# Attention plus feed-forward on one core: reordered ScalarE and VectorE work in the first tile, and moved steps of k and q

## The chip, the cores and the metric

The kernel runs on one core of a Trainium2 chip. TensorE multiplies, VectorE and ScalarE do the elementwise work, GpSimd takes a few elementwise steps, and SyncE issues the transfers. Each engine works through its own queue in order and waits at its head for what the next instruction needs. The metric is the device time of one execution in microseconds; 921.27 us is the median of three runs before the change (919.81 to 922.92).

## The reference

For each of 8 batches and 8 heads (576 positions, head size 64), `softmax` of q over the head dimension multiplies the matrix `softmax(k over positions)^T v`. The 4608 x 512 result x goes through a feed-forward layer of width 2048:

```
q_s = exp(q - max(q, -1)) / (sum(...) + 1e-9)          # over the 64 of a head
k_s = exp(k - max(k, axis=2)) / (sum(...) + 1e-9)      # over the 576 positions
x   = q_s @ (k_s^T v)                                  # per batch and head
h   = x @ w_in                                         # 4608x512 @ 512x2048
g   = max(h, 0) + log1p(exp(-|h|))                     # softplus
out = g @ w_out                                        # 4608x2048 @ 2048x512
```

All of it is fp32.

## The kernel before

**Tiles and slots.** The 4608 tokens are cut into nine tiles of 512 (`SUBS`), and the 2048 hidden columns into 16 blocks (`NJ`). A slot n is one pair (tile t, block j), n = 16 t + j. In a slot TensorE computes `up(t, j)` (L372 onwards) into a PSUM buffer `ph`, of which there are two, then `down` of the block two slots earlier into four accumulators `po`, then the products that other steps have left in the list `waiting`. Softplus of the slot (L387 to L402) is four ScalarE passes (|h|, exp, 1+u, ln) and three VectorE passes (L399 to L401). L400 reads `ph` and is the last reader of it, so `up` two slots on can overwrite the buffer only behind it.

**First tile.** In tile 0 matrices are multiplied in fp32: each matmul has two instructions in the trace, eight for an `up` and eight for a `down`. The weights come from memory as 64-bit words, and are put together while tile 0 runs, two blocks ahead: `top_w` (L122) and `scale_w` (L117) on ScalarE and `sign_w` (L128) on VectorE make the parts of block j+2 in slot j, `join_w` (L138) on VectorE joins those of block j+1 in slot j. `up` of a block needs its join. From tile 1 on the products are made of two rounded parts each (three matmuls for one); the weights are split for that once by `split_w` (L147 on ScalarE, L148 on VectorE), one block in each slot that `SPLITS` lists. The part of block k overwrites the raw words of block k-1, and block k must be split before slot 16+k. g is split in tile 1 and later by `split_g` (L406 on ScalarE, L407 on VectorE).

**Attention one tile ahead.** While tile t-1 runs, the steps of batch t and tile t are spread over its slots by `attend(t)`; `lazy(make, slots)` puts the i-th step of a unit in the slot that `slots` names. Lists `first`, `steps` and `last` hold what is issued in a slot: `first` and `steps` ahead of the split and of softplus, `last` behind softplus. For batches 1 and 2 (`ON_PE`) a unit of k and v is: `top` (L184, maximum over positions on VectorE, then a transpose on TensorE), `across` (L200, then a second transpose), `shift` (L205 on VectorE), `product` (exponential L211 on ScalarE, then 10 x 2 small matmuls L216 on TensorE), `scale` (L226, L227) and `split` (L240 on ScalarE, L243 on VectorE). There are two buffers `kvt` for k and v; the products of unit h release one, and behind them `kv_next` issues the load of the unit two further on (L169 and L172), whose `top` is the first to read it. The unit of q has twelve steps: two maxima (L280), a join, two shifts (L292), two exponentials (L295), two sums (L298), an inversion (L302, L303) and two divisions (L306). For tile 1 the shifts and divisions run on GpSimd, later on VectorE. The unit of x (L323, L329, L330, products L337 to L339, L349, L350) follows in the last slots of a tile.

**Order.** All of it stands under `tc.manual_schedule()`: each engine gets its instructions in the order in which the loop at the end of the function issues them.

Of the kernel before, what the change touches and what calls it, by code (L numbers as in the profile page):

```python
# [8 lines left out]
F32 = mybir.dt.float32  # L9
# [7 lines left out]
ALU = mybir.AluOpType  # L17
AX = mybir.AxisListType

P = 128  # L20
# [15 lines left out]
ON_PE = 2  # L36
START = [P * sum(SUBS[:t]) for t in range(len(SUBS) + 1)]
NTILE = len(SUBS)

SPLITS = [10, 11, 12, 13, 14, 15, 16, 17, 18, 19, 20, 21, 22, 23, 24, 25]  # L40
TOK = P * max(SUBS)
assert START[-1] == NT

# [13 lines left out]
def tile_attn_ffn(  # L57
# [9 lines left out]
    nc = tc.nc  # L67
# [4 lines left out]
    tp = ctx.enter_context(tc.tile_pool(name="tp", bufs=1))  # L72
# [15 lines left out]
    ln1 = const.tile([P, 1], F32, name="ln1")  # L88
# [7 lines left out]
    def load_w(k):  # L96
        raw[k] = wp.tile([P, 2, DM], I64, name=f"w{k}")
        nc.sync.dma_start(out=raw[k][:, 0], in_=w_in[k])
        nc.sync.dma_start(out=raw[k][:, 1], in_=w_out[k])
# [157 lines left out]
    def q_load(t):  # L257
        qt = qp.tile([P, HP * TOK], F32, name="qt")
        nc.sync.dma_start(out=qt, in_=q[:, HP * START[t]:HP * START[t + 1]])
        qtiles[t] = qt.rearrange("p (h n) -> p h n", h=HP)  # L260
# [126 lines left out]
    def softplus(t, j, ph):  # L387

        if t == 0:

            u, w = (tp.tile([P, TOK], F32, name=("u", "w", "l")[(2 * j + i) % 3]) for i in range(2))
            l = gp.tile([P, TOK], F32, name=("g_hi", "g_lo")[j % 2])
        else:
            u, w, l = (tp.tile([P, TOK], F32, name=name) for name in ("u", "w", "l"))
        nc.scalar.activation(u, ph, AF.Abs)  # L395
        nc.scalar.activation(u, u, AF.Exp, scale=-1.0)  # L396
        nc.scalar.activation(w, u, AF.Copy, bias=1.0)  # L397
        nc.scalar.activation(l, u, AF.Ln, bias=1.0)  # L398
        nc.vector.scalar_tensor_tensor(out=w, in0=w, scalar=1.0, in1=u, op0=ALU.subtract, op1=ALU.subtract)  # L399
        nc.vector.scalar_tensor_tensor(out=w, in0=ph, scalar=0.0, in1=w, op0=ALU.max, op1=ALU.subtract)  # L400
        nc.vector.scalar_tensor_tensor(out=l, in0=l, scalar=ln1, in1=w, op0=ALU.subtract, op1=ALU.add)  # L401
        return l  # L402

    def split_g(l):
        g_hi, g_lo = (gp.tile([P, TOK], F32R, name=name) for name in ("g_hi", "g_lo"))
        nc.scalar.copy(g_hi, l)  # L406
        nc.vector.tensor_tensor(out=g_lo, in0=l, in1=g_hi.bitcast(F32), op=ALU.subtract)  # L407
        return g_hi, g_lo
# [44 lines left out]
    def kv_prefetch(**place):  # L453
        if ahead[0] < len(kv_order):
            bh = kv_order[ahead[0]]
            loaded[bh] = kv_load(*bh, **place)
            ahead[0] += 1

    with tc.manual_schedule():

        make_identity(nc, ident)
        q_load(0)
        for i in range(HP):
            place = dict(pool=xp, tag=f"x{i - 1}", shape=(P, HP * TOK)) if i >= 2 else {}
            kv_prefetch(engine=nc.vector, queue=nc.scalar, **place)
        for k in range(5):
            load_w(k)
        nc.vector.memset(zero, 0.0)

        nc.scalar.activation(ln1, zero, AF.Ln, bias=1.0)  # L470
        whole = wp.tile([P, HP, P], F32, name="spare")
        qT = wp.tile([P, HP, TOK], F32, name=f"w{NJ - 1}")
        x0 = xp.tile([P, HP, TOK], F32, name="x0")
        for z in [whole] + [z.bitcast(F32) for i in range(2) for z in kv_hi[i] + kv_lo[i]]:
            nc.vector.memset(z, 0.0)

        po = [ps_o.tile([P, DM], F32, name=f"po{h}") for h in range(HP)]
        units = [kv_unit(0, h, po[h]) for h in range(HP)]  # L480
        first = [x_first(h, po[h]) for h in range(HP)]
        todo = {f"q{i}": fn for i, fn in enumerate(q_unit(0))}
        for h in range(HP):
            todo.update({f"u{h}{i}": fn for i, fn in enumerate(units[h])})
            todo.update({f"x{h}{i}": fn for i, fn in enumerate(first[h])})
        for k in range(3):
            for name, fn in (("t", top_w), ("m", scale_w), ("s", lambda k: sign_w(k, nc.gpsimd)), ("j", join_w)):
                todo[f"{name}{k}"] = lambda k=k, fn=fn: fn(k)

        warm = ps_h.tile([P, TOK], F32, name="ph")  # L490
        todo["warm"] = lambda: [nc.tensor.matmul(warm[:, 0:P], lhsT=ident, rhs=ident, start=True, stop=True) for _ in range(8)]
        todo["kv"] = kv_prefetch
        todo["w"] = lambda: [load_w(k) for k in range(5, 10)]
        todo["q"] = lambda: q_load(1)
        for name in (
            "q0 q1 u00 q2 q3 q4 q5 u10 u01 u11 u02 u12 q6 u03 u13 u20 u30 u21 u31 u22 u32 t0 m0 s0 u23 u33 warm q7 q8 q9 "
            "kv kv w u04 u14 u05 u15 q10 q11 x00 x10 x01 x11 t1 m1 u24 u34 u25 u35 x20 x30 x21 x31 s1 j0 x02 x12 x22 x32 "
            "t2 m2 s2 j1 q"
        ).split():
            todo[name]()  # L500

        def attend(t):

            steps = [[] for _ in range(NJ + 1)]
            first, last = ([[] for _ in range(NJ)] for _ in range(2))

            def lazy(make, slots):
                unit = []

                def step(i):  # L510
                    def fn():
                        if not i:
                            unit.extend(make())
                        unit[i]()
                    return fn

                for i, s in enumerate(slots):
                    where, s = s if isinstance(s, tuple) else (steps, s)
                    where[s].append(step(i))

            if t < B:
                for h in range(HP):
                    if t <= ON_PE:
                        slots = [2 * h + i for i in (0, 1, 2, 3, 4, 4)]
                    else:

                        g, z = 5 * (h // 2), h % 2
                        slots = [g + i for i in (z, z + 1, z + 1, 3, 4, 4)]
                    lazy(lambda h=h: kv_unit(t, h, banks[h % 2], after=kv_next), slots)
            lazy(lambda: q_unit(t), (3, 4, 5, 5, 6, 7, 8, 7, 8, 9, 9, 10) if t == 1 else (2, 3, 3, 4, 5, 6, 6, 7, 8, 8, 9, 10))  # L530
            for h in range(HP):
                a = h + 11
                lazy(
                    lambda h=h: x_unit(t, h, banks[h % 2]),
                    [a, a, a, a + 1 if h < 2 else NJ] if t == 1 else
                    [a, (last, a), (first, a + 1), (last, a + 1) if h < 2 else NJ],
                )
            if t + 1 < NTILE:
                steps[14].append(lambda: q_load(t + 1))
            return steps, first, last  # L540

        order = [(t, j) for t in range(NTILE) for j in range(NJ)]
        pending, soft, waiting = [], None, []
        for n in range(len(order) + 3):
            slot = order[n] if n < len(order) else None
            if slot:
                t, j = slot
                if j == 0:
                    steps, first, last = attend(t + 1) if t + 1 < NTILE else [[[] for _ in range(NJ + 1)]] * 3
                ph = up(t, j)  # L550
                if t == 0 and 1 < j + 1 < NJ:
                    join_w(j + 1)
                for fn in first[j] + steps[j]:
                    fn()
                if t == 0 and 1 <= j <= HP:
                    split_whole(j - 1)
                if n in SPLITS:
                    split_w(SPLITS.index(n))
                if j == NJ - 1:
                    for fn in steps[NJ]:  # L560
                        fn()
            if soft:
                pending.append((soft[0], split_g(soft[1]) if soft[0][0] else soft[1]))
                soft = None
            if slot:
                soft = slot, softplus(t, j, ph)
                if t == 0 and 2 < j + 2 < NJ:
                    for fn in (top_w, scale_w, sign_w):
                        fn(j + 2)
                for fn in last[j]:  # L570
                    fn()
            while pending and order.index(pending[0][0]) <= n - 2:
                (t, j), g = pending.pop(0)
                down(t, j, g)
            for products in waiting:
                products()
            waiting.clear()
# [37 lines left out]
```

## Time and profile before

| what | value |
|---|---|
| median of three runs | 921.27 us |
| the profiled execution, its own time | 920.85 us |
| its span, first to last instruction | 919.1 us |
| TensorE / VectorE / ScalarE / GpSimd busy | 883.2 / 700.7 / 582.7 / 67.0 us |
| granted TensorE clock, mean | 0.991 |

Times in a timeline are counted from the span's start. A row gives start and duration in us, the engine, the line of the kernel, the operation, what it writes and reads with shapes, the number of instructions merged in the row, and in square brackets how long the engine had been idle and what ended that. A start that comes a little before the end of the row ahead is the engine's pipeline.

### The profile page before, as it was taken

The numbers are of one execution on the slowest core, as the hardware profiler recorded it, in microseconds if no ns is written. First come the engines' busy times: TensorE is split into PE (matmuls) and PEld (weight loads), VectorE is DVE, ScalarE is ACT, GpSimd is POOL, SyncE is SP. The second block draws the span as 40 slices with busy tenths as digits, with TensorE's granted clock in tenths as the row PEclk, the third lists the DMA queues.
The fourth block names the chain that finished last, engine by engine and source line by source line (L and its number), as shares of the span: only waits on it lengthen the run. The fifth ranks groups of instructions, "written<-read, shape, count | busy, mean of one in ns | idle before, by whom it ended". The sixth has DMA issues, their size and how long they took to land.

```text
span 919.1 us, 11673 instructions
## 1 busy us (share of the span) xinstructions
PE 883.2 (96%) x4196; PEld 680.2 (74%) x4196; DVE 700.7 (76%) x1094; ACT 582.7 (63%) x982; POOL 67.0 (7%) x119
## 2 busy tenths in 40 slices
PE   3799989989999999999999999999999999999998
PEld 2343444667788888888888888888888888888886
DVE  8798878788778877887688768976897676765553
ACT  4666566767656665666576657665675566656554
POOL 2302300000000100020002000100110000000000
PEclk9899989999999999999999999999999999999999
DMA  9945101111013101301130113011200110001001
GB/s 313 381 141 195 52 0 47 46 53 32 21 46 98 36 17 47 98 23 30 46 98 9 44 46 98 1 52 46 84 16 1 46 47 1 1 1 47 0 1 46
DMA packets 49034, 55.28 MB, mean 60 GB/s; under 512 B 2256, under 2 KB 39120, under 8 KB 47824
## 3 DMA queue, kind: packets, MB, share of 16 engines
q1 hardware_dynamic: 48400, 54.27, 17.9%
q8 instruction: 33, 0.54, 0.2%
q10 hardware_dynamic: 576, 0.26, 0.1%
q14 instruction: 25, 0.20, 0.1%
HBM read 45.09 MB, written 9.44 MB: 59 GB/s over the span
## 4 chain that ended last, share of the span: by engine, by line
PE 83%; DVE 8%; ACT 5%; issue 2%; DMA 1%; POOL 0%; SPq 0%; DVEq 0%; ACTq 0%; POOLq 0%
PE ph L382 12%; PE po L427 12%; PE po L429 12%; PE po L428 12%; PE ph L383 12%; PE ph L384 12%; PE ph L377 3%; PE po L423 3%; PE att L216 2%; DVE w L138 1%; DVE w L128 1%; PE att L339 1%; PE att L338 1%; PE att L337 1%; DMA kvt<-in_kv_tail 1%
## 5 line engine op out<-in xcount | busy, mean ns | idle before, releaser
L429 PE MATMUL po<-w,g_lo 128*128 128x512 f32 x480 | 187.2, 390 | 1.9 <-DVE g_lo L407 1.9
L382 PE MATMUL ph<-x,w 128*128 128x512 f32 x480 | 188.8, 393 | 0.0
L427 PE MATMUL po<-w,g_hi 128*128 128x512 f32 x480 | 187.6, 391 | 0.0
L383 PE MATMUL ph<-x,w 128*128 128x512 f32 x480 | 186.9, 389 | 0.0
L428 PE MATMUL po<-w,g_hi 128*128 128x512 f32 x480 | 186.9, 389 | 0.0
L384 PE MATMUL ph<-x,w 128*128 128x512 f32 x480 | 186.8, 389 | 0.0
L399 DVE SCALAR_TENSOR_TENSOR w<-w,u 128x512 f32<-128x512 f32 x134 | 92.5, 690 | 117.1 <-ACT w L397 116.9
L406 ACT CAST g_hi<-l 128x512 fp32r<-128x512 f32 x128 | 79.5, 621 | 137.1 <-DVE l L401 134.9
L395 ACT ACTIVATE u<-ph 128x512 f32<-128x512 f32 x134 | 80.2, 598 | 55.6 <-PE ph L384 50.7
L401 DVE SCALAR_TENSOR_TENSOR l<-l,ln,w 128x512 f32<-128x512 f32 x128 | 96.3, 752 | 14.6
L429 PEld LDWEIGHTS po<-w,g_lo 128*128 128x128 f32 x480 | 90.1, 188 | 21.7 <-DVE g_lo L407 2.7
L382 PEld LDWEIGHTS ph<-x,w 128*128 128x128 f32 x480 | 90.4, 188 | 19.7 <-issue 0.6
L384 PEld LDWEIGHTS ph<-x,w 128*128 128x128 f32 x480 | 90.1, 188 | 19.0
L427 PEld LDWEIGHTS po<-w,g_hi 128*128 128x128 f32 x480 | 90.2, 188 | 18.0
L383 PEld LDWEIGHTS ph<-x,w 128*128 128x128 f32 x480 | 90.2, 188 | 17.9
L428 PEld LDWEIGHTS po<-w,g_hi 128*128 128x128 f32 x480 | 90.1, 188 | 17.8
L407 DVE TENSOR_TENSOR g_lo<-l,g_hi 128x512 fp32r<-128x512 f32 x128 | 87.1, 680 | 15.5 <-ACT g_hi L406 14.1
L400 DVE SCALAR_TENSOR_TENSOR w<-ph,w 128x512 f32<-128x512 f32 x134 | 92.6, 691 | 4.6
L397 ACT ACTIVATE w<-u 128x512 f32<-128x512 f32 x134 | 84.8, 633 | 4.2
L396 ACT ACTIVATE u<-u 128x512 f32<-128x512 f32 x134 | 84.7, 632 | 4.3
L398 ACT ACTIVATE l<-u 128x512 f32<-128x512 f32 x128 | 79.2, 619 | 12.5 <-DVE g_lo L407 12.5
L377 PE MATMUL ph<-x,w 128*128 128x512 f32 x128 | 61.6, 627 | 0.0
(136 smaller groups left out, 1020.7 us busy)
## 6 DMA issues: line engine op xcount, KB each, us to landing
kvt<-in_kv SPq DMA_DIRECT2D x30, 512.0 KB, 4.8
qt<-in_q SPq DMA_DIRECT2D x9, 1024.0 KB, 4.8
w<-in_w_in SPq DMA_DIRECT2D x16, 512.0 KB, 8.1
w<-in_w_out SPq DMA_DIRECT2D x16, 512.0 KB, 8.9
out<-w SPq DMA_DIRECT2D x32, 256.0 KB, 2.3
kvt<-in_kv_tail SPq DMA_DIRECT2D x28, 64.0 KB, 4.5
x<-in_kv SPq DMA_DIRECT2D x2, 512.0 KB, 9.4
out<-x SPq DMA_DIRECT2D x4, 256.0 KB, 2.4
```

The source lines that it names most:

```text
L377: nc.tensor.matmul(ph, lhsT=y[:, h * P:(h + 1) * P], rhs=x0[:, h], start=h == 0, stop=h == HP - 1)
L382: nc.tensor.matmul(ph, lhsT=w_hi, rhs=x_hi, start=h == 0, stop=False)
L383: nc.tensor.matmul(ph, lhsT=w_lo, rhs=x_hi, start=False, stop=False)
L384: nc.tensor.matmul(ph, lhsT=w_hi, rhs=x_lo, start=False, stop=h == HP - 1)
L397: nc.scalar.activation(w, u, AF.Copy, bias=1.0)
L399: nc.vector.scalar_tensor_tensor(out=w, in0=w, scalar=1.0, in1=u, op0=ALU.subtract, op1=ALU.subtract)
L400: nc.vector.scalar_tensor_tensor(out=w, in0=ph, scalar=0.0, in1=w, op0=ALU.max, op1=ALU.subtract)
L401: nc.vector.scalar_tensor_tensor(out=l, in0=l, scalar=ln1, in1=w, op0=ALU.subtract, op1=ALU.add)
L407: nc.vector.tensor_tensor(out=g_lo, in0=l, in1=g_hi.bitcast(F32), op=ALU.subtract)
L427: nc.tensor.matmul(po, lhsT=g_hi[:, ms], rhs=w_hi, start=j == 0, stop=False)
L428: nc.tensor.matmul(po, lhsT=g_hi[:, ms], rhs=w_lo, start=False, stop=False)
L429: nc.tensor.matmul(po, lhsT=g_lo[:, ms], rhs=w_hi, start=False, stop=j == NJ - 1)
```

## The change

It has five parts.

1. `SPLITS`: the sixteen weight splits go from slots 10 to 25 to slots 6 to 13, 16 to 19, 21, 23, 25 and 27.
2. In tile 0 softplus issues only L399 in its own slot; L400 and L401 (`rest`) are issued in the next slot, behind that slot's steps and split. The buffers are named accordingly: `u` is always the same one, `w` alternates between two.
3. In tile 0 the three conversions of block j+2 are issued ahead of softplus, and behind `rest` of the slot before.
4. For the k and v units of batches 1 and 2, `top` goes to the list `first` of its slot, and `shift` from slot 2h+2 to slot 2h+3, where the exponential is.
5. For q of tile 2 the steps' slots go from (2, 3, 3, 4, 5, 6, 6, 7, 8, 8, 9, 10) to (1, 2, 3, 4, 5, 5, 6, 6, 7, 8, 9, 10).

```diff
-SPLITS = [10, 11, 12, 13, 14, 15, 16, 17, 18, 19, 20, 21, 22, 23, 24, 25]
+SPLITS = [6, 7, 8, 9, 10, 11, 12, 13, 16, 17, 18, 19, 21, 23, 25, 27]
...
-            u, w = (tp.tile([P, TOK], F32, name=("u", "w", "l")[(2 * j + i) % 3]) for i in range(2))
+            u, w = (tp.tile([P, TOK], F32, name=name) for name in ("u", ("w", "l")[j % 2]))
...
         nc.vector.scalar_tensor_tensor(out=w, in0=w, scalar=1.0, in1=u, op0=ALU.subtract, op1=ALU.subtract)
-        nc.vector.scalar_tensor_tensor(out=w, in0=ph, scalar=0.0, in1=w, op0=ALU.max, op1=ALU.subtract)
-        nc.vector.scalar_tensor_tensor(out=l, in0=l, scalar=ln1, in1=w, op0=ALU.subtract, op1=ALU.add)
-        return l
+
+        def rest():
+            nc.vector.scalar_tensor_tensor(out=w, in0=ph, scalar=0.0, in1=w, op0=ALU.max, op1=ALU.subtract)
+            nc.vector.scalar_tensor_tensor(out=l, in0=l, scalar=ln1, in1=w, op0=ALU.subtract, op1=ALU.add)
+            return l
+
+        return rest
...
-                        slots = [2 * h + i for i in (0, 1, 2, 3, 4, 4)]
+                        slots = [(first, 2 * h)] + [2 * h + i for i in (1, 3, 3, 4, 4)]
...
-            lazy(lambda: q_unit(t), (3, 4, 5, 5, 6, 7, 8, 7, 8, 9, 9, 10) if t == 1 else (2, 3, 3, 4, 5, 6, 6, 7, 8, 8, 9, 10))
+            if t == 1:
+                slots = 3, 4, 5, 5, 6, 7, 8, 7, 8, 9, 9, 10
+            elif t <= ON_PE:
+                slots = 1, 2, 3, 4, 5, 5, 6, 6, 7, 8, 9, 10
+            else:
+                slots = 2, 3, 3, 4, 5, 6, 6, 7, 8, 8, 9, 10
+            lazy(lambda: q_unit(t), slots)
...
-                pending.append((soft[0], split_g(soft[1]) if soft[0][0] else soft[1]))
+                pending.append((soft[0], split_g(soft[1]) if soft[0][0] else soft[1]()))
                 soft = None
             if slot:
-                soft = slot, softplus(t, j, ph)
+
                 if t == 0 and 2 < j + 2 < NJ:
                     for fn in (top_w, scale_w, sign_w):
                         fn(j + 2)
+                l = softplus(t, j, ph)
+                soft = slot, l() if t else l
```

## Rows read from the trace of the kernel before

**Rows 1.** The head of the profile's page: the span, and busy time of each engine with its share and its instructions.

```profile
span 919.1 us, 11673 instructions
PE 883.2 (96%) x4196; PEld 680.2 (74%) x4196; DVE 700.7 (76%) x1094; ACT 582.7 (63%) x982; POOL 67.0 (7%) x119
```

**Rows 2.** The view of stretches, one of them in the third tile: its bounds and length, then busy time and instructions of TensorE, its weight loads, VectorE, ScalarE and GpSimd, granted clock, share of the DMA engines, GB/s.

```profile
300.00:400.00 100.00, 100.00 (x520) 83.04 (x519) 80.34 (x128) 65.47 (x114) 9.50 (x18) 1.00 0.14 45
```

**Rows 3.** The view of waits, TensorE only, whole span: who waited for whom, us in total, times, longest.

```profile
PE att L337 <- DVE q_lo L330: 5.6, 4, 2.6
PE att L186 <- DVE mx L184: 4.6, 3, 2.1
...
PE att L201 <- DVE m L200: 2.1, 1, 2.1
```

**Rows 4.** The timeline of TensorE in the first tile: `up` of slots 7, 8, 9 and 15 (L377), the transpose ahead of the first of them and the first product of x (L337) ahead of the last.

```profile
82.51 0.33 PE L186 MATMUL att<-ident,mx 128*128 128x128 f32 x1 [2.09 <-DVE mx L184]
82.67 5.30 PE L377 MATMUL ph<-x,w 128*128 128x512 f32 x8
...
92.40 3.60 PE L377 MATMUL ph<-x,w 128*128 128x512 f32 x8
...
99.44 3.59 PE L377 MATMUL ph<-x,w 128*128 128x512 f32 x8
...
153.33 0.30 PE L337 MATMUL att<-q_hi,kv_hi 128*128 128x64 f32 x1 [1.11 <-DVE q_lo L330]
...
154.38 3.60 PE L377 MATMUL ph<-x,w 128*128 128x512 f32 x8
```

**Rows 5.** The timeline of VectorE in the first tile: the joins (L138) of slots 1, 4, 5, 10, 11 and 14 (the first and the last of 14, among others), and L401 of slot 9.

```profile
41.20 1.22 DVE L138 SCALAR_TENSOR_TENSOR w<-w 128x1024 uint32<-128x1024 uint32 x1
...
59.70 1.23 DVE L138 SCALAR_TENSOR_TENSOR w<-w 128x1024 uint32<-128x1024 uint32 x1
...
69.39 1.23 DVE L138 SCALAR_TENSOR_TENSOR w<-w 128x1024 uint32<-128x1024 uint32 x1
...
107.43 1.47 DVE L401 SCALAR_TENSOR_TENSOR g_lo<-g_lo,ln,w 128x512 f32<-128x512 f32 x1
...
110.17 2.72 DVE L138 SCALAR_TENSOR_TENSOR w<-w 128x1024 uint32<-128x1024 uint32 x1
...
120.95 1.23 DVE L138 SCALAR_TENSOR_TENSOR w<-w 128x1024 uint32<-128x1024 uint32 x1
...
150.01 1.23 DVE L138 SCALAR_TENSOR_TENSOR w<-w 128x1024 uint32<-128x1024 uint32 x1
```

**Rows 6.** The timeline of GpSimd: the second division of q for tile 1.

```profile
108.88 2.93 POOL L306 TENSOR_TENSOR qt<-qt,s 128x1024 f32<-128x1024 f32 x1
```

**Rows 7.** The groups of VectorE's instructions in the first tile (33 to 160 us), shapes kept apart: count, busy us, mean ns of one, idle time before them.

```profile
L148 DVE TENSOR_TENSOR w<-w,w 128x1024 fp32r<-128x1024 f32 x5 | 6.1, 1223 | 1.3 <-ACT w L147 1.3
L184 DVE TENSOR_REDUCE mx<-kvt 128x128 f32<-128x640 f32 x4 | 5.2, 1302 | 0.0
...
L205 DVE TENSOR_TENSOR kvt<-kvt,att 128x640 f32<-128x640 f32 x4 | 3.3, 821 | 0.1
```

**Rows 8.** The page's list of costly groups: VectorE's three steps of softplus.

```profile
L399 DVE SCALAR_TENSOR_TENSOR w<-w,u 128x512 f32<-128x512 f32 x134 | 92.5, 690 | 117.1 <-ACT w L397 116.9
...
L401 DVE SCALAR_TENSOR_TENSOR l<-l,ln,w 128x512 f32<-128x512 f32 x128 | 96.3, 752 | 14.6
...
L400 DVE SCALAR_TENSOR_TENSOR w<-ph,w 128x512 f32<-128x512 f32 x134 | 92.6, 691 | 4.6
```

**Rows 9.** The timeline of ScalarE in slot 4: L240 of k's unit, the first pass of softplus, the two conversions.

```profile
61.28 0.63 ACT L240 ACTIVATE kv_hi<-att,r 64x64 fp32r<-64x64 f32 x2 [3.11 <-DVE r L227]
...
62.26 0.60 ACT L395 ACTIVATE l<-ph 128x512 f32<-128x512 f32 x1
...
64.61 1.13 ACT L122 ACTIVATE w<-w 128x1024 uint32<-128x1024 uint8 x1
65.64 1.15 ACT L117 ACTIVATE w<-w 128x1024 f32<-128x1024 f32 x1
```

**Rows 10.** The groups of ScalarE's instructions in the first tile, columns as in rows 7.

```profile
L147 ACT CAST w<-w 128x1024 fp32r<-128x1024 f32 x5 | 5.6, 1113 | 0.0
...
L211 ACT ACTIVATE kvt<-kvt 128x640 f32<-128x640 f32 x4 | 2.9, 729 | 0.0
...
L295 ACT ACTIVATE qt<-qt 128x1024 f32<-128x1024 f32 x2 | 2.1, 1049 | 0.0
```

**Rows 11.** The timeline of SyncE's queue: the second transfer of the load that unit 0 of batch 1 releases, and the first one of that which unit 0 of batch 2 releases.

```profile
58.62 0.67 SPq L172 DMA_DIRECT2D kvt<-in_kv_tail  x1
...
186.37 0.55 SPq L169 DMA_DIRECT2D kvt<-in_kv  x1
```

**Rows 12.** The view of transfers between 57.9 and 64 us: count, KB, us from issue to landing.

```profile
kvt<-in_kv_tail SPq DMA_DIRECT2D x1, 64.0 KB, 3.8
```

**Rows 13.** The timeline of VectorE in the second tile: the first instruction of slot 20's steps, k's maximum in that slot, L399 of slot 27, and the step behind that slot's softplus.

```profile
188.41 0.15 DVE L226 TENSOR_SCALAR r<-att 128x1 f32<-128x1 f32 x1
...
191.39 1.32 DVE L184 TENSOR_REDUCE mx<-kvt 128x128 f32<-128x640 f32 x1 [0.43 <-DMA kvt<-in_kv_tail]
...
239.77 0.69 DVE L399 SCALAR_TENSOR_TENSOR w<-w,u 128x512 f32<-128x512 f32 x1 [1.14 <-ACT w L397]
...
241.97 0.68 DVE L330 TENSOR_TENSOR q_lo<-att,q_hi 128x512 fp32r<-128x512 f32 x1
```

## The prediction

> **What bounds the kernel now.** I read the page's head first: TensorE is busy 883.2 of 919.1 us (96%), VectorE 700.7 [rows 1]. Then the stretches: from 300 to 400 us TensorE is busy all 100.00 us at clock 1.00 [rows 2]. Nothing in the diff reaches slots behind the second tile, so what can be won is TensorE's idle time in the first two tiles. The view of waits puts it at 5.6 + 4.6 + 2.1 = 12.3 us for three kinds of wait, every one ended by VectorE [rows 3]. A wait can cost more than itself: behind the wait of 2.09 us the eight passes of an `up` take 5.30 us instead of 3.60, which is half clock for part of them, 1.7 us more [rows 4]. The ceiling of any gain is thus some 14 to 18 us.
>
> So the first two tiles run at the pace of VectorE with ScalarE, and TensorE follows. I measure that pace by VectorE's rounds: from the start of one slot's join to the start of the next one's. From slot 1 to slot 14 the joins start at 41.20 and 150.01 [rows 5], 13 rounds in 108.81 us, in order 5.3, 6.8, 6.4, 9.7, 6.7, 9.9, 8.0, 9.2, 7.0, 10.8, 9.3, 9.9, 9.9. TensorE alone needs 7.04 us for a slot without attention (92.40 to 99.44 [rows 4]). Prices below are start to start, some 0.1 us under the durations of rows 7 to 10.
>
> **First tile, what is won.** In slot 0, L400 and L401 (0.69 + 0.75 [rows 8]) leave the place ahead of slot 1's join, which then starts at 39.7 instead of 41.2: 1.5 won. Slots 1 and 2 are shorter by 0.1 and 0.7 (k's shift goes out of slot 2, 0.82 [rows 7]).
>
> With the conversions first, the chain of a slot through ScalarE changes its end. Before, four passes and two conversions (62.26 to 65.64, and the second conversion's 1.1 [rows 9]) end in `sign_w`, some 1.3, and the join. After, conversions and three passes end in L399, 0.7, and the join. That is 0.5 (ln) + 0.6 = 1.1 less wherever the chain decides: slots 8 and 10 to 13. Slots 11, 12 and 13 become 8.2, 8.85, 8.85. Slot 10 (110.17 to 120.95, 10.78 [rows 5]) also loses the 1.5 by which its join is stretched (2.72 against 1.23): 8.0. Slot 8 takes a split's cast (1.05 [rows 10]) into the chain and stays at 9.1.
>
> **First tile, what it costs.** The maximum of k (L184) goes ahead of all other steps, and VectorE waits at its head for the load. In slot 4 that is the load issued behind the products of slot 3: its second transfer goes out at 58.62 [rows 11] and lands 3.8 later [rows 12], at 62.4. With TensorE 0.85 earlier that is 61.55, and VectorE is there at 59.8. The round of 9.69 loses the shift (0.74) and gains 1.75 of waiting: 10.7. In slots 3, 5, 7 and 9 the shift now stands in the slot of its exponential (0.73 [rows 10]), so ScalarE's queue, with conversions and softplus, waits behind VectorE. Slot 3: 1.14 join + 0.76 shift + 0.66 exponential + 0.3 cast of k^T v + 2.1 conversions + 1.95 three passes + 0.72 L399 = 7.65. Slot 5: GpSimd's shift of q holds L401, 8.2. Slot 6, with a split and without the shift: 9.9. Slot 7, as slot 3 with q's exponential (1.05 [rows 10]) and a cast of 1.05 for the one of 0.3: 9.5.
>
> Slot 9: its 7.0 loses a hold of 0.7 (L401 1.47 instead of 0.75 [rows 5, 8]) and gains a shift (0.74) and a split (1.12 [rows 7]). The split comes while GpSimd divides q. No row shows L148 beside GpSimd; the nearest are L401 and L138, two SBUF inputs each, and L138 ended 1.08 behind GpSimd's end (110.17 + 2.72 against 108.88 + 2.93 [rows 5, 6]). Its price lies between 0 and 2.2 (GpSimd's instruction from start to end); I take 2.1, as of L138. The round becomes 10.3. The Trainium skill ("SBUF — State Buffer", section "SBUF: two separate sides") says that a VectorE operation with two SBUF inputs and a GpSimd operation that reads SBUF exclude each other for a whole instruction. By that rule L148 is held and the sum stands; if only scalar_tensor_tensor were held, the first tile would end 2 us earlier.
>
> The 13 rounds: 5.2 + 6.1 + 7.65 + 10.7 + 8.2 + 9.9 + 9.5 + 9.1 + 10.3 + 8.0 + 8.2 + 8.85 + 8.85 = 110.55, so slot 14's join starts at 150.3, against 150.01.
>
> TensorE loses more, since L400 of a slot now comes in the next one, behind its steps and split, and the second `up` after it needs that `ph`. Bounds: nothing where VectorE is early, to 2.9 in a slot (L184's load, r, split ahead of L400, as in slot 6). L400 for slot 12 ends some 6.1 into slot 13's round, at 147.5; 7.04 and 1.05 for x's products (153.33 to 154.38 [rows 4]) put `up` of slot 15 at 155.7, against 154.38: 1.3 later. On the way TensorE waits 2 to 3 us ahead of slots 5, 7 and 10, where it can fall to half clock; VectorE's chain decides the slots behind, so I take that at nothing. If the cover is gone it costs 1.7 each.
>
> The earlier splits wait for nothing new: block k overwrites words that `down` of slot k+1 read, and its own slot is k+6. The products that issue the loads keep their slots, and so do the transposes behind L184, at a slot's end.
>
> **Second tile.** Splits leave slots 20, 22 and 24 and come to 27, two less from slot 20 to 27: -2.2. There VectorE's stretch was 188.41 to 241.97, 53.56 [rows 13]. The load for slot 20 goes out at 186.37 [rows 11] and VectorE has it at 191.39 with 0.43 of waiting [rows 13], because r, k^T v's low part and a shift come before. After, the maximum is first: VectorE would be there 1.8 behind the products' end and wait 3.2, +2.8. In slots 21, 23 and 25 ScalarE waits for the shift and then has k's exponential (0.66), in 21 q's (1.0), the cast (1.05), the rounding of g (0.55) and three passes (1.95). VectorE waits for the cast and for the third pass: 2.15 + 1.05 + 1.25 = +4.45. In slots 26 and 27 waits for ScalarE, such as 1.14 [rows 13], shrink by 1.2, since VectorE is late. Sum: -2.2 + 2.8 + 4.45 - 1.2, about +3.7 from slot by slot. q's steps are the same ones in these slots; that their start in slots 17 and 18 is earlier is hidden, as VectorE has room there (1.1 instead of 1.3 is carried into slot 20). TensorE then waits for the products of slots 21, 23 and 25, where the exponential is just done too late, and for x in slot 28. From there it is full.
>
> **Sum.** 1.1 + 3.7 = +4.8 on a span of 919.1 gives 923.9. The execution took 1.75 more than its span (920.85), 925.65; the median of the runs shown is 0.4 above it: 926.
>
> **Rivals.**
> Faster (25%): the shorter chain of slots 10 to 13 wins (-2.8 - 1.1 - 2.1 = -6.0), because the load of slot 4 is there when VectorE asks (-1.75) and GpSimd doesn't hold the split of slot 9 (-2.1). It decides from slot 10 on, if VectorE comes there no later than before: then slot 14's join starts at 146.4 and `up` of slot 15 at 151.8, 2.5 ahead. With that lead VectorE reaches the shifts of the second tile in time, the 4.45 don't come, and 3.7 becomes -0.75: 921.3 - 2.5 - 0.75 = 918. If slot 20's load is waited for no longer than before either (-2.8), 915. For it: less VectorE work in the second tile, and ScalarE is idle for long stretches (busy 63% [rows 1]). Against: row 191.39, where VectorE came 2 us into the slot and still had to wait for the load.
> Even (20%): the first tile as I have it (1.1 carried), and in the second ScalarE has the casts done before VectorE asks, so that of 3.7 the 4.45 are missing: 1.1 - 0.75, 921 to 922. TensorE's 96% speaks for little movement, the shift at the head of ScalarE's queue against it.
> Slower still (15%): TensorE falls from 2.4 to 1.2 GHz behind the longer waits. In the first tile VectorE's chain covers it; in slots 23 and 28 of the second (my estimates of the waits are 2.4 and 2.1) nothing does: 2 x 1.7 to 2.2, about 930. [...]
> My forecast has 40%, its own range is 923 to 929.
>
> A time within 0.3% (2.8 us) can't be told from no change here. Faster: 0.25. Same: 0.2. Slower: 0.55. For 8 in 10 I reach to the faster case and to the slower one: 915 to 931: below that all gains would have to come at once, above it half clock in three places.
>
> **What would show it.** Right: VectorE's L184 of slots 4 and 20 with a wait on the load of 1 to 3 us; TensorE's `up` in slots 5, 7, 9 and 10 waiting for L400; its L216 in slots 21, 23 and 25 waiting for L211; slot 14's join near 150; rounds 11 to 13 under 9. Wrong: joins well ahead of 148 at slot 14, or L216 without waits, or L148 of slot 9 at 1.2 beside GpSimd.

## The result, and the profile after

The changed kernel takes 926.39 us, median of 5 runs (924.77 to 930.24), against 921.35 (5 runs, 919.81 to 922.92) before: ratio 1.0057, 95% interval [1.0041, 1.0073]. The profiled execution took 927.62 us with a span of 925.8. The forecast was 926.0, in a range from 915 to 931, with slower as the likeliest sign. The time came out as forecast, but not all of the working did: two large terms of opposite sign were both too small, and that the median fell on the forecast itself is in good part luck. The experiments below take the two apart. One of the twelve executions of e10 below ran in a slow state (1273.76 us at a granted clock of 0.659) and is left out of its ratio; without it the median of e10 is 923.04.

The head of the page of the changed kernel, beside [rows 1]:

```profile
span 925.8 us, 11687 instructions
PE 885.2 (96%) x4196; PEld 681.1 (74%) x4196; DVE 698.2 (75%) x1094; ACT 582.1 (63%) x982; POOL 65.8 (7%) x119
```

The busy times hardly move; the loss is in waits. The view of waits of the changed kernel, TensorE only, whole span, columns as in [rows 3] (L400 to L407 of before are L402 to L411 here, and the `down` at L423 is L427):

```profile
PE ph L377 <- DVE l L402: 8.4, 4, 3.1
PE att L186 <- DVE kv_lo L243: 5.4, 4, 2.8
PE att L337 <- DVE q_lo L330: 2.4, 1, 2.4
PE att L216 <- issue: 2.2, 2, 1.2
```

Of before's three kinds of wait [rows 3] the one for x's parts (L337) falls from 5.6 to 2.4. The other two give way to new ones: `up` waits for the delayed L402, and the transposes wait for k^T v's low part. VectorE in the first tile of the changed kernel shows how the first of these arises (slot 1's join, then slots 4 to 6, and slot 14's join):

```profile
39.95 1.22 DVE L138 SCALAR_TENSOR_TENSOR w<-w 128x1024 uint32<-128x1024 uint32 x1
...
57.78 1.22 DVE L138 SCALAR_TENSOR_TENSOR w<-w 128x1024 uint32<-128x1024 uint32 x1
62.27 1.28 DVE L184 TENSOR_REDUCE mx<-kvt 128x128 f32<-128x640 f32 x1 [3.26 <-DMA kvt<-in_kv_tail]
...
66.61 0.69 DVE L402 SCALAR_TENSOR_TENSOR l<-ph,l 128x512 f32<-128x512 f32 x1
...
77.18 1.21 DVE L138 SCALAR_TENSOR_TENSOR w<-w 128x1024 uint32<-128x1024 uint32 x1
81.59 1.30 DVE L184 TENSOR_REDUCE mx<-kvt 128x128 f32<-128x640 f32 x1 [3.20 <-DMA kvt<-in_kv_tail]
...
151.75 1.22 DVE L138 SCALAR_TENSOR_TENSOR w<-w 128x1024 uint32<-128x1024 uint32 x1
```

At 57.78 + 1.22 = 59.0 VectorE has nothing left but what stands behind the maximum, and the maximum waits 3.26 us at the head of the queue for the load. Everything behind it, L402 at 66.61 among it, is later by that, and `up` of slot 5 waits for L402. TensorE at that place (the transpose and `up` of slot 5, then `up` of slots 11 and 15):

```profile
65.20 0.33 PE L186 MATMUL att<-ident,mx 128*128 128x128 f32 x1 [0.48 <-DVE kv_lo L243]
67.36 5.28 PE L377 MATMUL ph<-x,w 128*128 128x512 f32 x8 [1.83 <-DVE l L402]
...
123.88 5.41 PE L377 MATMUL ph<-x,w 128*128 128x512 f32 x8 [3.10 <-DVE l L402]
...
157.61 3.59 PE L377 MATMUL ph<-x,w 128*128 128x512 f32 x8
```

Behind such waits the eight passes take 5.28 and 5.41 us instead of 3.60 [rows 4]: part of them ran at the lower of the two clock levels (granted clock 0.96, 0.96 and 0.95 in the stretches from 33, 81 and 120 to 155 us). Slot 15's `up` starts at 157.61 instead of 154.38 [rows 4], 3.2 later. In the second tile TensorE waits twice for k^T v's low part and twice for the exponential (the view of waits calls that "issue"), and the first product of x in slot 28 comes at 249.47:

```profile
197.08 0.33 PE L186 MATMUL att<-ident,mx 128*128 128x128 f32 x1 [1.83 <-DVE kv_lo L243]
...
212.35 0.33 PE L186 MATMUL att<-ident,mx 128*128 128x128 f32 x1 [2.84 <-DVE kv_lo L243]
...
219.20 0.80 PE L216 MATMUL att<-kvt 128*64 128x65 f32 x20 [1.03 <-issue]
...
232.45 0.80 PE L216 MATMUL att<-kvt 128*64 128x65 f32 x20 [1.20 <-issue]
...
249.47 0.33 PE L337 MATMUL att<-q_hi,kv_hi 128*128 128x128 f32 x1 [2.38 <-DVE q_lo L330]
```

In the kernel before that product stood here:

```profile
242.71 0.33 PE L337 MATMUL att<-q_hi,kv_hi 128*128 128x128 f32 x1 [1.46 <-DVE q_lo L330]
```

From that row to the end of the span it is 919.1 - 242.71 = 676.4 before and 925.8 - 249.47 = 676.3 after. So the start of this product measures what differs between two versions (but for e5 and e11, see there), and slot 14's join divides it into a first-tile and a second-tile part. The first tile lost 151.75 - 150.01 = 1.7, of which 0.35 was there at slot 0's join, and the second 97.7 - 92.7 = 5.0, together 6.8 in the profiled pair (the medians differ by 5.0). All versions are read in these numbers, the median of all executions and three from one trace each:

| version | median us | slot 14's join | from slot 0's join to slot 14's | from slot 14's join to x's product in slot 28 |
|---|---|---|---|---|
| before | 921.35 to 922.10 | 150.01 | 115.79 | 92.70 |
| after | 926.39 | 151.75 | 117.18 | 97.72 |
| e4: k's moves alone | 941.05 | 159.52 | 125.01 | 101.81 |
| e1: after, maximum not first | 919.64 | 144.92 | 111.52 | 95.43 |
| e2: after, shift as before | 918.07 | 146.30 | 111.34 | 93.11 |
| e3: after, k as before | 909.28 | 141.93 | 108.52 | 89.09 |
| e5: after, two loads ahead | 922.61 | 145.15 | 110.61 | 97.62 |
| e6: parts 2 and 3 alone | 909.62 | 135.39 | 102.60 | 94.39 |
| e7: part 3 alone | 921.86 | 151.36 | 116.91 | 93.05 |
| e10: part 2 alone | 923.12 | 152.59 | 116.34 | 93.68 |
| e8: part 1 alone | 920.98 | 151.59 | 118.46 | 89.67 |
| e11: e6, two loads ahead | 910.39 | 136.74 | 103.39 | 93.76 |
| e9: e3, two loads ahead | 909.18 | 141.77 | 107.11 | 89.79 |
| e12: e6, late splits later | 906.04 | 136.26 | 101.81 | 90.84 |

The runs of the kernel before beside the experiments had medians of 922.10 (with e1 to e4), 921.75 (e5 to e8), 921.85 (e9 to e11) and 921.55 (e12); intervals below are of ratios to these. The column of slot 14's join holds the start-up too, which differs between the traces (slot 0's join from 32.8 to 36.3); the column behind it doesn't, and is the one to compare first tiles by.

### The profile page after: what moved, and what is told of

Read it like the earlier page. It is cut to its first block, busy times and chain, and to the rows that moved or that the text cites. A ratio compares the mean times of both kernels' runs of the same rounds, so it can differ in the third digit from the quotient of the medians.

```text
span 925.8 us, 11687 instructions
## 1 busy us (share of the span) xinstructions
PE 885.2 (96%) x4196; PEld 681.1 (74%) x4196; DVE 698.2 (75%) x1094; ACT 582.1 (63%) x982; POOL 65.8 (7%) x119
## 4 chain that ended last, share of the span: by engine, by line
PE 86%; DVE 5%; ACT 4%; issue 2%; DMA 2%; POOL 0%; SPq 0%; ACTq 0%; DVEq 0%; POOLq 0%
PE ph L382 12%; PE po L431 12%; PE po L433 12%; PE ph L384 12%; PE po L432 12%; PE ph L383 12%; PE ph L377 4%; PE po L427 4%; PE att L216 2%; DMA kvt<-in_kv_tail 1%; PE att L339 1%; PE att L338 1%; PE att L337 1%; ACT u L396 1%; PE po L361 1%
## 5 line engine op out<-in xcount | busy, mean ns | idle before, releaser
L399 DVE SCALAR_TENSOR_TENSOR w<-w,u 128x512 f32<-128x512 f32 x136 | 94.2, 693 | 116.7 <-ACT w L397 116.0
L395 ACT ACTIVATE u<-ph 128x512 f32<-128x512 f32 x144 | 86.0, 598 | 55.4 <-PE ph L384 50.1
L403 DVE SCALAR_TENSOR_TENSOR l<-l,ln,w 128x512 f32<-128x512 f32 x128 | 96.3, 752 | 15.0 <-DVE w L402 0.5
L411 DVE TENSOR_TENSOR g_lo<-l,g_hi 128x512 fp32r<-128x512 f32 x128 | 87.1, 681 | 15.4 <-ACT g_hi L410 14.1
L402 DVE SCALAR_TENSOR_TENSOR w<-ph,w 128x512 f32<-128x512 f32 x136 | 94.0, 691 | 4.4
L396 ACT ACTIVATE u<-u 128x512 f32<-128x512 f32 x144 | 91.0, 632 | 4.6
L377 PE MATMUL ph<-x,w 128*128 128x512 f32 x128 | 63.1, 640 | 9.0 <-DVE l L402 8.4
```

The costliest lines, as they stand in the source:

```text
L377: nc.tensor.matmul(ph, lhsT=y[:, h * P:(h + 1) * P], rhs=x0[:, h], start=h == 0, stop=h == HP - 1)
```

## Experiments

### Which of k's moves costs (e1 to e4)

k's slots in the changed kernel are `[(first, 2*h)] + [2*h + i for i in (1, 3, 3, 4, 4)]`. Three variants of the changed kernel take back one move or both, and e4 makes only these moves (part 4), in the kernel before.

```diff
-                        slots = [(first, 2 * h)] + [2 * h + i for i in (1, 3, 3, 4, 4)]
# e1
+                        slots = [2 * h + i for i in (0, 1, 3, 3, 4, 4)]
# e2
+                        slots = [(first, 2 * h)] + [2 * h + i for i in (1, 2, 3, 4, 4)]
# e3
+                        slots = [2 * h + i for i in (0, 1, 2, 3, 4, 4)]
```

> The changed kernel, but k's maximum goes back behind the scale and split of the unit two before it, in the same slot (the shift stays with the exponential). Theory A, the load at the head of VectorE's queue: slots 4, 6 and 20 have waits of 3.3, 3.2 and 2.0 us there, and the transposes behind it gain nothing since they wait for the low part of k^T v; with 1.7 us of that work ahead of the wait, about 1.7 comes back in each of them, 921 to 923. Theory B, the shift at the head of ScalarE's queue: no change, 925 to 927. Theory C, the cost is in the first tile's softplus order and earlier splits: no change, 925 to 927.

> The changed kernel, but the shift goes back one slot ahead of its exponential (the maximum stays first). Theory A: VectorE still waits for the load first, and the shift comes on top of that in the full slots, 925 to 928. Theory B: ScalarE has the exponential, the casts and softplus ready earlier in slots 3, 5, 7, 9, 21, 23 and 25, the waits of TensorE for the products (1.0 and 1.2 us) go, 922 to 924. Theory C: 925 to 927.

> The changed kernel with both moves of k undone; the splits, the softplus order, the conversions and q of the third batch stay as changed. Theories A and B together: the cost of 5 us goes and what the shorter chain of slots 10 to 13 wins remains, 915 to 920. Theory C: 924 to 927.

> The kernel before with the two moves of k alone. Theories A and B: slower than before by 4 to 7 us, 925 to 928. Theory C: the moves of k cost little by themselves, 920 to 922.

Measured: e1 919.64 us (0.9973 [0.9959, 0.9988]), e2 918.07 (0.9956 [0.994, 0.9973]), e3 909.28 (0.9858 [0.9836, 0.988]), e4 941.05 (1.0196 [1.017, 1.0222]). The two moves of k cost 926.39 - 909.28 = 17.1 us in the changed kernel and 941.05 - 922.10 = 19.0 in the kernel before. From e3, the maximum first alone (e2) costs 8.8 and the late shift alone (e1) 10.4: they nearly add up. The rest of the change wins 12.8. My working had neither a gain nor a loss of this size, and all four times lie outside every range that was expected of them: e1 gains more than theory A said, e2 more than B, and e3 and e4 show the sign of A and B at about three times the size. Theory C, softplus and splits as the cost, is refuted by e3 and e4.

The late shift shows in the rounds of the slots where it now stands: in e1 slots 3, 5, 7 and 9 take 7.45, 7.47, 9.26 and 10.69, in e3 5.79, 6.72, 6.73 and 9.63. Half of that comes back in slots 2, 4, 6 and 8, which the shift has left (3.1 less in e1), so the first tile is 3.0 longer in e1 than in e3, and 2.8 in e2. The larger part lies in the second tile, 6.3 in e1 and 4.0 in e2: from slot 14's join to x's product TensorE is idle for 4.7 us in e1, 4.0 in e2 and 1.5 in e3, and the rest is a longer busy time (90.77, 89.14 and 87.63 us) at a mean granted clock of 0.98, 0.98 and 1.00. In e4 the first tile is 9.2 longer than before, though VectorE waits only 0.80 there for a load: slots 3, 5, 7 and 9 take 8.80, 9.48, 9.53 and 9.93 instead of 6.35, 6.68, 8.00 and 7.02, so in the kernel before it is the late shift that costs in this tile. The maximum first shows where its load is late. VectorE in slots 4 and 6 of e2 and of e3:

```profile
62.64 1.28 DVE L184 TENSOR_REDUCE mx<-kvt 128x128 f32<-128x640 f32 x1 [4.17 <-DMA kvt<-in_kv_tail]
...
81.11 1.30 DVE L184 TENSOR_REDUCE mx<-kvt 128x128 f32<-128x640 f32 x1 [2.44 <-DMA kvt<-in_kv_tail]
```

```profile
58.57 0.82 DVE L205 TENSOR_TENSOR kvt<-kvt,att 128x640 f32<-128x640 f32 x1
61.05 1.30 DVE L184 TENSOR_REDUCE mx<-kvt 128x128 f32<-128x640 f32 x1 [1.66 <-DMA kvt<-in_kv_tail]
...
76.28 0.82 DVE L205 TENSOR_TENSOR kvt<-kvt,att 128x640 f32<-128x640 f32 x1
77.83 1.33 DVE L184 TENSOR_REDUCE mx<-kvt 128x128 f32<-128x640 f32 x1 [0.73 <-DMA kvt<-in_kv_tail]
```

In e3 the shift and other steps fill the time in which the load is under way; the waits are 1.66 and 0.73 instead of 4.17 and 2.44, and no `up` of the first tile takes more than 3.71 us (mean granted clock 1.000 in e3, 0.993 in after).

That the moved maximum gains TensorE nothing is seen in the releasers. In e1, with the maximum at its old place, the one long wait of the second tile's transposes is ended by the maximum; with it first (after, e2, e4) they are ended by L243:

```profile
204.62 0.39 PE L186 MATMUL att<-ident,mx 128*128 128x128 f32 x1 [2.77 <-DVE mx L184]
```

Units two apart share a PSUM bank for their transposes and k^T v (`banks[h % 2]`), and L243 is the last reader of the earlier unit, so the transpose can't start before it, however early the maximum is. The Trainium skill ("PSUM — Partial Sum Buffer", section "PSUM bank collisions raise a hardware error") asks for a guard between engines by bank, not by address. No run here tells the two apart, since the transpose also writes the columns that L243 reads (`bank[:, 0:P]` and `bank[:, 0:D + 1]` in `kv_unit`).

### Whether the load is what the early maximum pays for (e5)

The loads of units 2 and 3 of batch 1 go out at the start into two buffers of x that are idle then, and behind the products of these two units nothing is loaded. Units 0 and 1 still release a load each, now that of units 0 and 1 of batch 2 (issued at 57.49 and 72.66 instead of 96.94 and 113.53).

```diff
+        for i in (1, 2):
+            todo[f"kx{i}"] = lambda i=i: kv_prefetch(pool=xp, tag=f"x{i}", shape=(P, HP * TOK))
...
-            "kv kv w u04 u14 u05 u15 q10 q11 x00 x10 x01 x11 t1 m1 u24 u34 u25 u35 x20 x30 x21 x31 s1 j0 x02 x12 x22 x32 "
+            "kv kv kx1 kx2 w u04 u14 u05 u15 q10 q11 x00 x10 x01 x11 t1 m1 u24 u34 u25 u35 x20 x30 x21 x31 s1 j0 x02 x12 x22 x32 "
...
-                    lazy(lambda h=h: kv_unit(t, h, banks[h % 2], after=kv_next), slots)
+                    lazy(lambda h=h: kv_unit(t, h, banks[h % 2], after=None if t == 1 and h > 1 else kv_next), slots)
```

> The changed kernel, with k and v of the third and fourth unit of batch 1 loaded at the start into two x buffers that are idle until slot 12, so that the maxima of slots 4 and 6 have nothing to wait for; the order of the steps is the changed one. Theory A, the load at the head of VectorE's queue: the waits of 3.3 and 3.2 us in slots 4 and 6 go, and what follows from them (TensorE's waits ahead of slots 5 and 7 and their half clock): 6 to 8 us less than the changed kernel, 918 to 921. Rival B, the shift at the head of ScalarE's queue decides the first tile: at most 2 us less, 924 to 926.

Measured: 922.61 (1.0011 [1.0002, 1.002]), 3.8 less than the changed kernel, between the two expectations, and so outside both. In the first tile theory A holds: slots 4 and 6 take 8.61 and 9.20 instead of 11.96 and 12.48, and slot 14's join comes 6.6 earlier. The second tile, in which slot 20's load is waited for as before (2.05 against 2.04), stays at 97.62. x's product comes 6.7 earlier, but 1.7 of it is given back behind it (920.8 - 242.77 = 678.0 instead of 676.3): a wait of 2.37 ahead of that product, and behind it passes of 0.63 us where 0.39 is usual, in a stretch with clock 0.97 where the changed kernel has 1.00. The stretch from 240 to 300 us, first of e5, then of the changed kernel, columns as in [rows 2]:

```profile
240.00:300.00 60.00, 57.63 (x289) 47.58 (x288) 45.22 (x72) 36.93 (x67) 3.33 (x9) 0.97 0.17 55
```

```profile
240.00:300.00 60.00, 57.62 (x296) 47.81 (x295) 46.62 (x74) 39.55 (x71) 2.97 (x8) 1.00 0.15 50
```

### What wins the 12 us (e6, e7, e10, e8)

e6 is the kernel before with parts 2 and 3, e7 with part 3 alone (conversions ahead of softplus, all three VectorE steps at their place), e10 with part 2 alone (two steps a slot later, conversions behind softplus), e8 with the new `SPLITS` alone.

```diff
# e7
-                soft = slot, softplus(t, j, ph)
                 if t == 0 and 2 < j + 2 < NJ:
                     for fn in (top_w, scale_w, sign_w):
                         fn(j + 2)
+                soft = slot, softplus(t, j, ph)
# e10, in e6
-                if t == 0 and 2 < j + 2 < NJ:
-                    for fn in (top_w, scale_w, sign_w):
-                        fn(j + 2)
                 l = softplus(t, j, ph)
                 soft = slot, l() if t else l
+                if t == 0 and 2 < j + 2 < NJ:
+                    for fn in (top_w, scale_w, sign_w):
+                        fn(j + 2)
# e8
-SPLITS = [10, 11, 12, 13, 14, 15, 16, 17, 18, 19, 20, 21, 22, 23, 24, 25]
+SPLITS = [6, 7, 8, 9, 10, 11, 12, 13, 16, 17, 18, 19, 21, 23, 25, 27]
```

> The kernel before with the new softplus order of the first tile alone: conversions first, two VectorE steps a slot later. Theory P, the chain from ScalarE's first work of a slot to the next join is 1.1 us shorter (L399 ends it instead of the sign): most of the 13 us that the changed kernel wins without its moves of k, 910 to 915. Theory R, the win is the splits': 919 to 923.

> The kernel before with the conversions ahead of softplus, and all of softplus's VectorE steps still in their own slot. By the chain of theory P: conversions 2.1, three passes 1.95, then three VectorE steps 2.2 ahead of the join, 6.2 against 5.8 before: no win, 921 to 926. If the conversions' place alone is what wins: 910 to 916.

> The kernel before with the new slots of the weight splits alone. Theory P: in slots 6 to 9 a split's cast comes into a chain that is already full, in the second tile VectorE has less to do: both small, 919 to 925. Theory R: the splits are what wins, 908 to 914.

> The kernel before with part 2 alone: VectorE's L400 and L401 a slot later in tile 0, conversions still behind softplus on ScalarE. The conversions ahead of softplus alone had won nothing (921.86), both together 12 us (909.62). Theory P (the last link to end decides a round): here the chain still runs through four passes, two conversions, sign_w and join (2.5 + 2.1 + 1.3 + 1.1 a slot), so only slot 0's 1.5 and GpSimd's hold of slot 10 go: 917 to 921, slot 14's join at 146 to 150. Rival Q (the two steps were VectorE work in front of the join, and taking them away wins whatever ScalarE does): near the two together, 908 to 912, join near 136.

Measured: e6 909.62 (0.987 [0.9855, 0.9886]), e7 921.86 (1.0001 [0.9988, 1.0015]), e10 923.12 (1.0012 [0.9998, 1.0025]), e8 920.98 (0.9988 [0.9978, 0.9998]). Each of parts 2 and 3 alone is worth nothing, both together 12 us. The end of slot 13 on VectorE says why. In e7 the conversions are done early, but three softplus steps stand between the third ScalarE pass and the join:

```profile
149.16 0.69 DVE L399 SCALAR_TENSOR_TENSOR u<-u,l 128x512 f32<-128x512 f32 x1 [0.47 <-ACT u L397]
149.89 0.69 DVE L400 SCALAR_TENSOR_TENSOR u<-ph,u 128x512 f32<-128x512 f32 x1
150.69 0.75 DVE L401 SCALAR_TENSOR_TENSOR g_lo<-g_lo,ln,u 128x512 f32<-128x512 f32 x1
151.36 1.22 DVE L138 SCALAR_TENSOR_TENSOR w<-w 128x1024 uint32<-128x1024 uint32 x1
```

In e10 VectorE has done its softplus steps, and waits for the conversion behind four passes before `sign_w` (L128) and the join:

```profile
149.36 0.68 DVE L399 SCALAR_TENSOR_TENSOR l<-l,u 128x512 f32<-128x512 f32 x1
151.24 1.31 DVE L128 TENSOR_SCALAR w<-w 128x1024 uint8<-128x1024 uint8 x1 [1.20 <-ACT w L117]
152.59 1.23 DVE L138 SCALAR_TENSOR_TENSOR w<-w 128x1024 uint32<-128x1024 uint32 x1
```

In the first tile of e10 that wait comes eight times, 10.0 us in total. In e6 neither is there, and the join follows on L399:

```profile
133.45 1.32 DVE L128 TENSOR_SCALAR w<-w 128x1024 uint8<-128x1024 uint8 x1
134.78 0.69 DVE L399 SCALAR_TENSOR_TENSOR l<-l,u 128x512 f32<-128x512 f32 x1
135.39 1.22 DVE L138 SCALAR_TENSOR_TENSOR w<-w 128x1024 uint32<-128x1024 uint32 x1
```

Two chains of nearly equal length end in slot 14's join. From ScalarE's first pass or conversion of slot 13 to the join it is 5.9 us before (144.10 to 150.01, through the conversions) and in e10 (146.69 to 152.59), 6.2 in e7 (145.16 to 151.36, through VectorE's three steps) and 4.6 in e6 (130.79 to 135.39). Shortening one chain leaves the other, or lengthens it; with both short, TensorE itself is the bound. The first tile of e6 in stretches, columns as in [rows 2]:

```profile
81.00:120.00 39.00, 39.00 (x131) 17.99 (x130) 35.33 (x52) 29.14 (x41) 4.70 (x8) 1.00 0.19 66
120.00:155.00 35.00, 35.00 (x98) 17.56 (x97) 28.55 (x36) 24.84 (x36) 0.00 (x0) 1.00 0.08 31
```

TensorE is busy in all 74 us at full clock. e6 is 0.4 below theory P's range, and theory R, the splits, falls with e6 and e8. e10's time is above theory P's 917 to 921, and its join of slot 14 at 152.59 is behind 146 to 150. 2.0 of that is its later start (slot 0's join at 36.25 against 34.22). The two credits came, 1.6 in slot 0 and 1.5 in slot 10, but slot 1 is 1.6 longer, as `sign_w` waits 1.88 there for the conversion, and slot 9 is 2.0 longer, as GpSimd holds `sign_w` there (below); so the first tile wins nothing. Rival Q, 908 to 912, falls. e8 moves time from the second tile to the first: +2.7 (118.46 against 115.79) and -3.0.

### Loads ahead without k's moves, and a better version (e11, e9, e12)

e11 is e6, e9 is e3, each with e5's edit. e12 is e6 with the six splits of slots 20 to 25 in slots 21, 23, 25, 27, 28 and 29.

```diff
# e12
-SPLITS = [10, 11, 12, 13, 14, 15, 16, 17, 18, 19, 20, 21, 22, 23, 24, 25]
+SPLITS = [10, 11, 12, 13, 14, 15, 16, 17, 18, 19, 21, 23, 25, 27, 28, 29]
```

> The kernel before with parts 2 and 3, and the loads of units 2 and 3 of batch 1 issued at the start into two spare buffers, no reload behind the units' products for those. With k's moves that load had been worth 3.8 us. Theory A (the load's price came only from the maximum being first): with k's slots as before VectorE waits 2.34 for slot 4's load once and nothing in slot 6, so it gains 0 to 1.5 on 909.6: 908 to 910. Rival B (the load bounds the first tile anyway): 905 to 907.

> The changed kernel with k's slots as before, and the loads of units 2 and 3 of batch 1 issued at the start. The changed kernel with k's slots as before ran 909.28. Theory A: 907.5 to 909.5, since VectorE's waits for those loads there were 1.66 and 0.73 and part of that is hidden. Rival B: 905 to 907.

> The kernel before with parts 2 and 3, and the six last splits (slots 20 to 25) in slots 21, 23, 25, 27, 28 and 29, where VectorE waits 0.7 to 2.0 us a slot for ScalarE; the splits of the first tile stay. Parts 1 and 5 shortened the second tile (slot 14's join to x's product in slot 28) from 94.39 to 89.09 but lengthened the first by as much. Theory T (VectorE sets the pace of both tiles, a split costs wherever VectorE has no room): x's product comes 2 to 5 us earlier, 905 to 908. Rival U (the second tile's pace is set by TensorE's own waits for k's transposes, not by splits): 909 to 910.

Measured: e11 910.39 (0.9879 [0.9857, 0.99]), e9 909.18 (0.9865 [0.9841, 0.9889]), e12 906.04 (0.9835 [0.9821, 0.9848]). Loads ahead are worth nothing where k's slots are as before: theory A both times (e11 0.4 above its range; behind x's product it gives back 1.7 as e5 does, 908.5 - 230.50 = 678.0, so up to that much may be hidden). Parts 1 and 5 are worth nothing beside 2 and 3 (e3 and e6 agree within 0.4): the second tile is 5.3 shorter in e3, the first 5.9 longer, all of it and more in slots 6 to 9, where the early splits are (35.3 in e3, 28.7 in e6). Part 5 was never run without part 1. e12 leaves the early splits out and keeps the free slots of the second tile: from slot 14's join to x's product it takes 90.84 instead of e6's 94.39. That is theory T, and it is the fastest version, 1.65% below the kernel before.

## Why the prediction was right, and where it wasn't

**Slot 0.** Slot 1's join at 39.7 predicted, 39.95 measured, in an execution that started its first `up` 0.35 later. Right.

**Shorter chain in slots 8 and 10 to 13.** Predicted 9.1, 8.0, 8.2, 8.85, 8.85; measured 8.92, 7.97, 8.01, 8.60, 8.64. Right to 0.25. But the credit was for these slots alone; e6 shows slots 6 and 7 shorter by 1.8 and 2.4 as well, once k's moves and the early splits are away (with the splits, in e3, slot 6 is no shorter and slot 7 by 1.3). Of slot 6's 1.8, 1.5 is its join, which GpSimd stretched before as it did slot 10's (76.07, 2.73 us in the trace before; 1.22 in e6); I credited that in slot 10 alone. This is the part of the 12 us that I didn't see: I added k's moves and a split to those slots before asking what the new order alone would do there.

**Late shift in slots 3, 5 and 7.** Predicted 7.65, 8.2, 9.5; measured 7.46, 7.44, 9.24. Right in slots 3 and 7; slot 5 is 0.8 shorter than predicted, though GpSimd's shift of q did hold L403 (L401 of before) there, 1.83 us instead of 0.75.

**Load of slot 4.** Predicted a wait of 1.75 and a round of 10.7; measured 3.26 and 11.96. Right in kind, too small by 1.5: VectorE was there at 59.0 instead of 59.8, the load went out at 58.11 instead of 57.8, and took 4.2 instead of 3.8 until VectorE had it.

**Slot 6.** Predicted 9.9, measured 12.48: the largest error of the first tile, and the step of the prediction that failed there. I took half clock behind the waits for `ph` "at nothing", since VectorE's chain decides the slots behind. It doesn't where a load hangs on TensorE. `up` of slot 5 started after 1.83 of waiting and took 5.28; behind it the products, behind these the next load, behind that the maximum of slot 6 with 3.20 of waiting. SyncE's queue of the changed kernel has that load (the one of slot 4 went out at 58.11):

```profile
77.64 0.67 SPq L172 DMA_DIRECT2D kvt<-in_kv_tail  x1
```

**Slot 9 and GpSimd.** The forecast was that L148 is held for 2.1. It wasn't: it started together with the division and took 1.23, which was one of the three signs of being wrong. The hold fell on the next VectorE operations with two SBUF inputs. VectorE, then GpSimd, of the changed kernel:

```profile
111.59 1.23 DVE L148 TENSOR_TENSOR w<-w,w 128x1024 fp32r<-128x1024 f32 x1
112.73 0.68 DVE L402 SCALAR_TENSOR_TENSOR w<-ph,w 128x512 f32<-128x512 f32 x1
113.45 1.68 DVE L403 SCALAR_TENSOR_TENSOR g_hi<-g_hi,ln,w 128x512 f32<-128x512 f32 x1
115.06 1.32 DVE L128 TENSOR_SCALAR w<-w 128x1024 uint8<-128x1024 uint8 x1
116.18 2.43 DVE L399 SCALAR_TENSOR_TENSOR l<-l,u 128x512 f32<-128x512 f32 x1
```

```profile
111.59 3.00 POOL L306 TENSOR_TENSOR qt<-qt,s 128x1024 f32<-128x1024 f32 x1 [13.01 <-ACT w L147]
...
115.11 2.94 POOL L306 TENSOR_TENSOR qt<-qt,s 128x1024 f32<-128x1024 f32 x1
```

L403 (0.75 alone [rows 8]) and L399 (0.69) each end some 0.55 behind the end of a division: 113.45 + 1.68 = 115.13 against 114.59, and 116.18 + 2.43 = 118.61 against 118.05. That is (1.68 - 0.75) + (2.43 - 0.69) = 2.7 instead of 2.1, and more than the upper bound of 2.2; the round came out at 10.71 instead of 10.3. L402, with one input in PSUM, isn't held. L128, with one input, started 0.05 ahead of the second division; in e10, where it started 0.55 behind the start of one, it took 3.02 (111.19), so one input alone isn't what frees it. What the rows point to for L148 is its start: it isn't that only scalar_tensor_tensor is held, as a TENSOR_TENSOR of VectorE of the same size took 2.69 us instead of 1.22 in the trace before when it started 0.31 behind a division of GpSimd (L306, 24.69 and 24.38), and in e2, e3, e8 and e9 L148 started 0.23 ahead of the division and took 1.16. By the Trainium skill ("SBUF — State Buffer", section "SBUF: two separate sides") whichever of the two engines starts first has the pair of ports for its whole instruction. The rows with two SBUF inputs agree with that; the prediction drew on the rule, but put L148 on the losing side.

**`up` of slot 15.** Predicted 1.3 later than before, measured 3.2, of which 0.35 was there at the start. The waits for `ph` came ahead of slots 5, 7, 9 and 11 (5, 7, 9 or 10 predicted); the one ahead of 11 was the longest, 3.10 with half clock behind it.

**Second tile.** Predicted +3.7 from VectorE's start in slot 20 (the four figures add up to 3.85), measured +3.1 there. What was too small is the delay carried into slot 20: 1.1 predicted, 3.7 measured (VectorE there at 192.07 against 188.41), so that from slot 14's join to x's product it is +5.0. The load of slot 20 was waited for 2.04 instead of 3.2. The term for the shift was right in kind: at 219.20 TensorE waited 1.03 for the products of slot 23, whose exponential ended at 219.11, 1.20 in slot 25 and not at all in slot 21, and at 249.47 for x with 2.38 (my estimate was 2.1). What I had wrong is a sentence in the costs: that the transposes keep their place, at a slot's end, which I gave no price. They wait for L243, 1.83 and 2.84 here.

**The sum.** +4.8 predicted, +6.8 in the profiled pair, +5.0 in the medians. The terms for k's moves were too small (17 us by e3), and so was the term for softplus (12 us by e6); the errors cancelled, and that the median came within 0.4 of the forecast is luck to that extent. The faster rival asked for a load in time and an early lead; both were missing, 3.26 and 3.20 of waiting in slots 4 and 6. Its time of 918 is reached with either of k's moves taken back (918 to 920), but that is another kernel. The even rival fell with the second tile's +5.0. The rival of half clock in the second tile didn't occur in the changed kernel, where 2.38 ahead of slot 28's product was followed by passes of 0.39 us; it did in e5, for 1.7 us, as priced, and from slot 14's join to x's product the granted clock is 0.98 in e1, e2 and e5 and 0.95 in e4, against 1.00 in the changed kernel.

## What to carry to other kernels

Where two chains of about the same length end in one instruction, shortening one of them shows nothing; try both together before either is dropped. On an engine that works in order, an instruction that waits for a load, as k's maximum here, belongs behind the work that is ready, even where its own result is wanted early, and moving it up helps nobody if the reader of its result waits for something else. A change whose parts were only run together should be run part by part: here 12 us of gain lay under 17 us of loss.

## What was not expected

The same wait can cost its own length or nearly double. Behind 3.10 us ahead of slot 11 the eight passes took 5.41 us in the changed kernel; in e3 2.12 at the same place left them at 3.71, and in e9 2.09 was followed by 5.41; in the second tile 2.38 cost nothing more in the changed kernel, and behind 1.74 in e11 passes took 0.63 us instead of 0.39. What tells these apart was not tried. And the start-up alone differs by 3.5 us between two traces with the same code up to there (slot 0's join at 32.79 in e6, at 36.25 in e10), so in single traces the first tile is to be read from rounds, not from places.
